# Attention heads with backward pass: the loads of K, V and wo on Activation's queue at written places, and half of the scale factors of Q made by VectorE

## The chip, the cores and the metric

The program runs on one core of a Trainium2 chip. It has a matrix engine (TensorE, PE in the rows of the profile), three engines for element-wise work (VectorE or DVE, Activation or ACT, GpSimd or POOL), and SyncE (SP), which issues transfers. DMAs are issued by SyncE, Activation or POOL; each has a queue of its own, and all run on the same sixteen DMA engines of the core. In the profile q1 is SyncE's queue, q0 POOL's and q10 Activation's. The metric is the device time of one execution in microseconds (us).

## The reference

One forward and backward pass of a block: layer norm of x (2048 rows of 576), attention of 32 heads over a cached K and V (2048 rows of 128 per head), a gated unit of width 4608, and their product added to x. All gradients are wanted.

```python
def _A_ref(x, k_cache, v_cache, wq, wo):
    q = (x @ wq).reshape(B, Sq, H, Dh).transpose(0, 2, 1, 3)
    scores = einsum("bhqd,bhkd->bhqk", q, k_cache) * (Dh ** -0.5)
    p = softmax(scores)
    o = einsum("bhqk,bhkd->bhqd", p, v_cache)
    return o.transpose(0, 2, 1, 3).reshape(B, Sq, H * Dh) @ wo
...
    xn = _layernorm(x)
    s = _A_ref(xn, k_cache, v_cache, wq, wo)
    g = silu(_B_ref(xn, w_gate, w_up, w_down))
    return x + s * g
```

The change lies in the attention heads. For each head the kernel computes the scores S = Q K^T, P = exp(S - max), the output O = P V divided by the sum of each row, dP = dO V^T, dS = P (dP - delta), and from them dQ = dS K, dK = dS^T Q and dV = P^T dO.

## The kernel before

The kernel first does the layer norm and the gated unit, then the 32 heads one after the other, then the products with wo, the gradients of the weights and dx. The heads are one long list of steps with positions, written by hand: `at(position, function, arguments)`. A head is 64 positions long, called halves (`HEAD`); head h starts at 64 h (`b`), and `back(x)` is position x of the head before. In halves 0 to 31 the score tiles are made, two halves for each of 16 blocks of 128 query rows (`s_half`, on VectorE line 523; `s_exp`, line 533); in halves 32 to 63 the tiles of dP and dS (`dp_half`, lines 554 to 560; `ds_mul`, line 564). These are the anchors; all else is put between them and overlaps with the next head.

The list is sorted and run through once. For TensorE, VectorE and Activation its order is the order in which they work (`MAN`). POOL and SyncE are not in `MAN`: a scheduler of the framework places their instructions, so the position of a step that POOL carries out says only where it stands in the list.

Within a head:

- `trans_P` and `trans_dS` turn pairs of finished blocks of P and dS by a DMA transpose that SyncE issues (line 568), 16 per head, into four buffers (`wpt`). The matmuls of `row_mm` (line 597) read them, in groups of four blocks: P with `Vn` from half 16.8 + 8 g on, dS with `Kn` from half 48.8 + 8 g on, so that the last two groups of dS run in the first halves of the next head.
- `kv_mm` (line 621) makes dV from P and the scaled dO (`dOn`), and dK from dS and the scaled Q (`Qn`). dV's two passes come first.
- `prep_kt` and `prep_vt` turn K and V on TensorE (line 485). K of the next head is turned at halves 37.2 and 40.0, V at halves 0.2 and 10.4 of its own head, eight of its sixteen blocks each time.
- `prep_wo` (lines 465 and 466) turns the head's part of wo at half 52.2 of the head before; `proj` makes Q and dO of the head from wq, wo and the inputs.
- `q_scale` multiplies Qn by 1/sum and the constant `SCALE`, eight blocks at a time, at halves 24.5 and 43.3: first the factors `rsc` (line 510, 128 x 8 numbers), then the product (line 511). Both run on POOL.
- `o_sink` finds delta: a product on POOL, its sum on VectorE, `negdelta` on POOL (line 657), which Activation uses in the first half of each block's dP (line 560).
- POOL also issues the stores of dV, dK, O and dQ (lines 634, 637, 659 and 669), 16 per head of 128 KB each.

The loads for the next head stand at `back(20.0)` (wq, line 449, and wo_h, line 454) and `back(35.1)` (K, line 425, and V, line 438), all issued by POOL. `Kn` has two buffers, used by even and odd heads; `Vn` and `wo_h` have one. So K waits for the last dQ matmul of the head before last, V for the last P V matmul of the head, wo_h for `prep_wo`. Head 0 has its K and V loaded in halves during the phase before (`LOADS`), line 419. In the last head Activation loads the rest of wo (`load_wo`, line 401), 15 DMAs.

Of the kernel before, what the change touches and what calls it, by code (L numbers as in the profile page):

```python
# [14 lines left out]
P = 128  # L15
# [81 lines left out]
def kernel(  # L97
# [6 lines left out]
    nc = tc.nc  # L104
# [6 lines left out]
    NT = S // P  # L111
# [8 lines left out]
    SCALE = float(Dh) ** -0.5  # L120
# [69 lines left out]
    wo_h = pk.tile([P, D], bf, name="wo_h")  # L190
# [186 lines left out]
    def bcast(v, n):  # L377
        return v.unsqueeze(2).to_broadcast([P, n, P])
# [4 lines left out]
    def at(pos, fn, *args):  # L383
        prog.append((pos, len(prog), fn, args))

    def anchor(pos, fn, *args):
        anchors.append((pos, len(anchors), fn, args))
# [25 lines left out]
            self.PT = [None] * NT  # L413
            self.dST = [None] * NT

    def load_part(dst, src, k):
        for k_ in range(2) if k is None else (k,):
            ts = slice(k_ * NT // 2, (k_ + 1) * NT // 2)
            nc.gpsimd.dma_start(dst[:, ts, :], src.rearrange("(p t) d -> p t d", t=NT)[:, ts, :])

    def load_k(hs, k=None):
        if not k:
            hs.Kn = (late["ldK2"] if hs.h % 2 else ldK).tile([P, NT, P], bf, name="Kn")
        if k is None:
            nc.gpsimd.dma_start(hs.Kn[:], A_k_cache[0, hs.h].rearrange("(p t) d -> p t d", t=NT))
        else:
            load_part(hs.Kn, A_k_cache[0, hs.h], k)

    def load_v(hs, k=None):
        if not k:  # L430
            hs.Vn = ld1.tile([P, NT, P], bf, name="Vn")
            hs.rs_all = hstat.tile([P, NT], f32, name="rs_all")
            hs.rinv_all = hstat.tile([P, NT], f32, name="rinv_all")
            hs.delta = hstat.tile([P, NT], f32, name="delta")
            hs.negdelta = hstat.tile([P, NT], f32, name="negdelta")
            hs.rsc = hstat.tile([P, NT], f32, name="rsc")
        if k is None:
            nc.gpsimd.dma_start(hs.Vn[:], A_v_cache[0, hs.h].rearrange("(p t) d -> p t d", t=NT))
        else:
            load_part(hs.Vn, A_v_cache[0, hs.h], k)  # L440

    def load_kv(hs):
        load_k(hs)
        load_v(hs)

    def load_wq(hs):
        hc = slice(hs.h * P, (hs.h + 1) * P)
        hs.wq = wh.tile([P, DT, P], bf, name="wq_h", bufs=1)
        nc.gpsimd.dma_start(hs.wq[:, :DL, :], A_wq[:DL * P, hc].rearrange("(t p) c -> p t c", p=P))
        nc.gpsimd.dma_start(hs.wq[:KL, DL, :], A_wq[DL * P:, hc])  # L450
        nc.gpsimd.memset(hs.wq[KL:, DL, :], 0.0)

    def load_wo_h(hs):
        nc.gpsimd.dma_start(wo_h[:], A_wo[hs.h * P:(hs.h + 1) * P, :])

    def load_w(hs):
        load_wq(hs)
        load_wo_h(hs)

    def prep_wo(hs, eng):  # L460
        hs.woT = wh.tile([P, DT, P], bf, name="woT_h", bufs=1)
# [45 lines left out]

    def q_scale(hs, g):
        gs = slice(g * 8, (g + 1) * 8)
        nc.gpsimd.tensor_scalar(hs.rsc[:, gs], hs.rinv_all[:, gs], SCALE, None, op0=ALU.mult)  # L510
        nc.gpsimd.tensor_tensor(hs.Qn[:, gs, :], hs.Qn[:, gs, :], bcast(hs.rsc[:, gs], 8), op=ALU.mult)

    def s_half(hs, qt, hf):
# [88 lines left out]
    def rows(pos, hs, T, rhs, g, sinks, w):  # L602
        bx = Box()
        sink, after = sinks
        for j in range(GQ):
            for kt in range(NT):
                at(pos + w * (j * NT + kt) / (GQ * NT - 1), row_mm, bx, hs, T, rhs, g * GQ + j, kt, sink)
        if after:
            at(pos + w + (DELTA1 if g == 1 else AFTER), after)
# [33 lines left out]
    def o_sink(hs, g):  # L643
        gs = slice(g * GQ, (g + 1) * GQ)
        bx = Box()

        def sink(acc):
            bx.ou = late["wt"].tile([P, GQ, P], bf, name="ou", bufs=1)
            alt.copy(bx.ou[:], acc[:], eng=OUE)
            bx.prod = late["wt"].tile([P, GQ, P], f32, name="prod", bufs=1)  # L650
            nc.gpsimd.tensor_tensor(bx.prod[:], bx.ou[:], hs.dOn[:, gs, :], op=ALU.mult)

        def after():
            prod, ou = bx.prod, bx.ou
            o_n = late["stg"].tile([P, GQ, P], bf, name="o_n", bufs=1)
            nc.vector.tensor_reduce(hs.delta[:, gs], prod[:], axis=AX.X, op=ALU.add)
            nc.gpsimd.tensor_scalar(hs.negdelta[:, gs], hs.delta[:, gs], -1.0, None, op0=ALU.mult)
            nc.gpsimd.tensor_tensor(o_n[:], ou[:], bcast(hs.rinv_all[:, gs], GQ), op=ALU.mult)
            nc.gpsimd.dma_start(on2_d[g * CH:(g + 1) * CH, hs.h * P:(hs.h + 1) * P].rearrange("(t p) d -> p t d", p=P), o_n[:])

        return sink, after
# [127 lines left out]
    HEAD = 2 * H1  # L789
    XR, ROW_W, ROW_W2, DELTA1 = 16.8, 6.7, 6.15, 5.7  # L790
    KVE, OUE = ("vs", "ss"), "s"
    WOT_AT = 52.2
    QT_AT, DOT_AT = ((32.6, 47.2, 55.2, 60.2), "s"), ((2.2, 6.2, 14.2, 18.2), "s")
    KT_AT, DON_AT, VT_AT, QN_AT = (37.2, 40.0, "s"), (8.9, 22.0, "v"), (0.2, 10.4, "s"), (24.2, 28.2, "s")
    PSTEP, QS_AT = 0.4, (24.5, 43.3)
# [7 lines left out]
    def adds(pos, w):  # L803
        load_[int(pos * FINE) % (HEAD * FINE)] += w
# [3 lines left out]
    for j in range(DT):  # L808
        adds(WOT_AT, 1)
    for p_ in KT_AT[:2] + DON_AT[:2] + VT_AT[:2] + QN_AT[:2]:  # L810
# [54 lines left out]
    for h in range(H):  # L865
        hs = Head(h) if h else first
        b = h * HEAD
        back = lambda x: b - HEAD + x
        if h:
            at(back(20.0), load_w, hs)  # L870
            at(back(35.1), load_kv, hs)
        for c in range(NCH):
            for i in range(DT):
                if h:
                    at(back(QT_AT[0][c] + PSTEP * i), proj, hs, "QT", c, i, QT_AT[1])
                at(b + (DOT_AT[0] if h else DOT_0)[c] + PSTEP * i, proj, hs, "dOT", c, i, DOT_AT[1])
        if h:
            at(back(WOT_AT), prep_wo, hs, "s")
        for g in range(2):
            if h:  # L880
                at(back(KT_AT[g]), prep_kt, hs, g, KT_AT[2])
            at(b + (DON_AT if h else DON_0)[g], prep_don, hs, g, DON_AT[2])
            at(b + (VT_AT if h else VT_0)[g], prep_vt, hs, g, VT_AT[2])
            at(b + QN_AT[g], prep_qn, hs, g, QN_AT[2])
            at(b + QS_AT[g], q_scale, hs, g)
        for p in range(NT // 2):
            at(b + 4 * p + 2 + RINV_AT, s_rinv, hs, p)
            at(b + max(4 * p + 2.1 + RINV_AT, DON_AT[p // 4] + 0.5), s_scale, hs, p)
        for qt in range(NT):
            p1, p2 = b + 2 * qt, b + H1 + 2 * qt  # L890
            for hf in range(NHF):
                anchor(p1 + hf, s_half, hs, qt, hf)
                anchor(p2 + hf, dp_half, hs, qt, hf)
            at(p1 + EXP_AT, s_exp, hs, qt)
            if qt % 2:
                if h == H - 1 and qt - 1 in P_PE:
                    for i, p_ in enumerate(P_PE[qt - 1]):
                        at(b + p_, pe_pair, hs.PT, hs.Pp, qt - 1, "PT", 8, ps_tr, "tr", i, "s")
                else:
                    at(p1 + PT_AT if h else max(p1 + PT_AT, LATE_AT + 0.1), trans_P, hs, qt - 1)  # L900
                if h == H - 1 and qt - 1 in DS_PE:
                    for i, p_ in enumerate(DS_PE[qt - 1]):
                        if len(DS_PE[qt - 1]) == 4:
                            at(b + p_, pe_pair, hs.dST, hs.dSp, qt - 1, "dST", 8, ps_tr, "tr", i, "s")
                        else:
                            at(b + p_, pe_pair, hs.dST, hs.dSp, qt - 1, "dST", NT, late["ps_big"], "big", i, "sv"[i])
                else:
                    at(p2 + DST_AT, trans_dS, hs, qt - 1)
            if qt not in STT2:
                at(p2 + DSM_AT, ds_mul, hs, qt)  # L910
        for g in range(NG):
            rows(b + 8 * g + XR + (0 if h or g else O0), hs, hs.PT, "Vn", g, o_sink(hs, g), ROW_W - (0 if h or g else O0))
            rows(b + H1 + 8 * g + XR, hs, hs.dST, "Kn", g, dq_sink(hs, g), ROW_W2 if g == 2 else ROW_W)
        for half, (pv, pk_) in enumerate(((VA, KA), (VB, KB))):
            kv(b, pv, hs, hs.P, "dOn", half, dvT_d, out_3)
            kv(b, pk_, hs, hs.dS, "Qn", half, dkT_d, out_2)
# [18 lines left out]
    if True:  # L935
# [84 lines left out]
        with tc.tile_pool(name="b1o", bufs=2, reuse_waits="tile") as outp, tc.tile_pool(name="b1t", bufs=3, reuse_waits="tile") as tmpp, \  # L1020
# [17 lines left out]
            class halves:  # L1038
                n, t = 0, None
# [298 lines left out]
```

## Time and profile before

| | us |
|---|---|
| three runs | 4982.95, 4999.9, 5007.65 |
| median | 4999.9 |
| the profiled execution | 4992.16 |
| its span, from the first to the last instruction | 4990.4 |

The granted clock of TensorE over the span is 0.997. Of the parts, the heads take the most: the first score tile of head 0 is worked on at 452.3 us, the last matmul of the last head's dQ starts at 3603.1 us.

How to read the rows: an engine's busy time is the sum of its instructions; a row of instructions has the line in the kernel, the engine, the operation, output and inputs by their names, the count, busy time and mean duration, and in a timeline the start and the duration in us, with the idle time before it and what ended it in brackets. A row of windows has for each engine the busy time and in brackets the number of instructions. A row of one line's instructions gives shortest, median and longest in ns and the first and last start in us.

### The profile page before, as it was taken

The page shows a single profiled execution, that of the slowest core. Times are in us where ns is not written, and L with a number is a line of the kernel's source. Part 1 is how long each engine was busy: PE and PEld are TensorE (multiplying, and loading weights), DVE is VectorE, ACT ScalarE, POOL GpSimd, SP SyncE. Part 2 cuts the span into 40 slices and gives each one's busy share as a digit, 9 for nine tenths or more (in the row PEclk, how much of TensorE's full clock was granted, in tenths as well). Part 3 has the DMA queues.
Part 4 walks back from the last instruction along what each step waited for, and adds up shares of the span by engine and source line. Part 5 has one row for each costly group of instructions (what it writes and reads, how often), then busy time and mean ns, then how long its engine had stood idle before and what let it go on. Part 6 is the DMA issues. An engine that isn't in the chain of part 4 may idle for free.

```text
span 4990.4 us, 103082 instructions
## 1 busy us (share of the span) xinstructions
PE 4886.3 (98%) x43022; PEld 3079.7 (62%) x43760; DVE 3072.9 (62%) x4844; ACT 2475.2 (50%) x3135; POOL 1543.3 (31%) x2206
## 2 busy tenths in 40 slices
PE   9999999999999999999999999999999999999999
PEld 3445776666666666666666666666657777655554
DVE  6545878888887888888787887887632222110111
ACT  5534666766666676676666666766502222100000
POOL 4323333333343333334333333333323332211000
PEclk9999999999999999999999999999999999999999
DMA  7887999999999999999999999999999989999898
GB/s 258 279 221 153 206 206 209 209 213 207 206 214 213 210 208 207 206 208 207 209 211 202 210 209 202 206 209 204 224 202 258 248 230 249 279 271 240 185 229 196
DMA packets 2879845, 1086.91 MB, mean 218 GB/s; under 512 B 2685360, under 2 KB 2808240, under 8 KB 2879376
## 3 DMA queue, kind: packets, MB, share of 16 engines
q1 hardware_dynamic: 2789728, 789.32, 87.9%
q0 software_dynamic: 85440, 286.38, 20.1%
q8 instruction: 342, 5.60, 0.5%
q10 hardware_dynamic: 4208, 4.57, 0.4%
q14 instruction: 127, 1.04, 0.1%
HBM read 172.54 MB, written 231.41 MB: 81 GB/s over the span
## 4 chain that ended last, share of the span: by engine, by line
PE 81%; DMA 8%; issue 1%; DVE 0%; ACT 0%; POOL 0%; DVEq 0%; ACTq 0%; POOLq 0%
PE acc L597 18%; PE acckv L621 14%; PE sp L521 8%; PE acc L1266 8%; PE dp L554 7%; DMA dST<-dSq 5%; PE accw L1119 5%; PE accp L478 5%; PE accd L1093 3%; PE dh L1065 2%; PE acc L1185 2%; PE acc L1001 2%; PE acct L485 2%; PE accq L1196 2%; PE acckv L618 2%
## 5 line engine op out<-in xcount | busy, mean ns | idle before, releaser
L533 ACT ACTIVATE Pq<-sneg,nm 128x2048 bf16<-128x2048 bf16 x512 | 1025.7, 2003 | 227.4 <-DVE sneg L523 190.1
L597 PE MATMUL acc<-Kn,dST 128*128 128x128 bf16 x8192 | 937.8, 220 | 39.0 <-DMA dST<-dSq 23.9
L557 DVE SCALAR_TENSOR_TENSOR dSq<-dp,delta,Pq 128x1024 bf16<-128x1024 f32 x544 | 694.7, 1282 | 374.8 <-PE dp L554 371.9
L597 PEld LDWEIGHTS <-dST 128*128 128x128 bf16 x8192 | 669.5, 98 | 397.0 <-DMA dST<-dSq 32.8
L597 PE MATMUL acc<-Vn,PT 128*128 128x128 bf16 x8192 | 899.1, 219 | 13.2 <-DMA PT<-Pq 2.7
L597 PEld LDWEIGHTS <-PT 128*128 128x128 bf16 x8192 | 652.0, 98 | 348.5 <-DMA PT<-Pq 5.1
L560 ACT ACTIVATE t<-dp,negdelta 128x1024 bf16<-128x1024 f32 x480 | 535.1, 1115 | 487.5 <-PE dp L554 477.6
L523 DVE TENSOR_SCALAR_CACHE_REDUCE sneg<-sp,nm 128x1024 bf16<-128x1024 f32 x512 | 656.5, 1282 | 114.8 <-PE sp L521 98.7
L523 DVE TENSOR_SCALAR_CACHE_REDUCE sneg<-sp 128x1024 bf16<-128x1024 f32 x512 | 625.2, 1221 | 98.6 <-PE sp L521 54.1
L554 PE MATMUL dp<-VT,dOT 128*128 128x512 bf16 x1988 | 597.9, 380 | 3.0 <-DVE dSq L557 0.3
L521 PE MATMUL sp<-KT,QT 128*128 128x512 bf16 x1960 | 590.7, 379 | 3.4 <-DVE sneg L523 2.8
L621 PE MATMUL acckv<-dSq,Qn 128*128 128x512 bf16 x1739 | 587.9, 380 | 0.4 <-ACT kv L41 0.3
L621 PE MATMUL acckv<-Pq,dOn 128*128 128x512 bf16 x1681 | 553.5, 379 | 1.7 <-POOL dOn L541 0.3
L564 DVE TENSOR_TENSOR dSq<-t,Pq 128x1024 bf16<-128x1024 bf16 x480 | 377.6, 787 | 0.0
L541 POOL TENSOR_TENSOR dOn<-dOn,rinv_all 128x256 bf16<-128x256 bf16 x256 | 157.1, 614 | 368.3 <-DVE rinv_all L537 317.2
L1119 PEld LDWEIGHTS <-xn_all 128*128 128x128 bf16 x2304 | 224.2, 98 | 28.1 <-DMA xn_all<-xn_d 0.4
L1282 DVE SCALAR_TENSOR_TENSOR junk<-dxn,xn_all 128x576 f32<-128x576 f32 x16 | 12.1, 758 | 362.5 <-ACT dxn L1277 362.5
L1266 PEld LDWEIGHTS <-cf 128*128 128x128 bf16 x2304 | 145.5, 98 | 136.8 <-DMA wqT<-in_A_wq_dram 0.2
L521 PEld LDWEIGHTS <-QT 128*128 128x128 bf16 x2048 | 169.7, 98 | 95.9 <-issue 6.1
L554 PEld LDWEIGHTS <-dOT 128*128 128x128 bf16 x2048 | 169.9, 98 | 95.2 <-issue 5.8
L478 PE MATMUL accp<-xnT,wq_h 128*128 128x512 bf16 x612 | 220.4, 381 | 0.1
L1277 ACT ACTIVATE dxn<-acc 128x512 f32<-128x512 f32 (+1 forms) x32 | 12.8, 406 | 394.9 <-issue 302.1
(217 smaller groups left out, 7272.4 us busy)
## 6 DMA issues: line engine op xcount, KB each, us to landing
h_d<-h_row POOLq DMA_DIRECT2D x48, 384.0 KB, 2.7
a_d<-a_row POOLq DMA_DIRECT2D x48, 384.0 KB, 3.5
b_d<-b_row POOLq DMA_DIRECT2D x48, 384.0 KB, 4.5
a_blk<-a_d SPq DMA_DIRECT2D x18, 1024.0 KB, 6.4
b_blk<-b_d SPq DMA_DIRECT2D x18, 1024.0 KB, 21.8
out_dram<-turn SPq DMA_DIRECT2D x35, 512.0 KB, 4.0
h_blk<-h_d POOLq DMA_DIRECT2D x17, 1024.0 KB, 15.9
on_d<-o_n POOLq DMA_DIRECT2D x128, 128.0 KB, 6.4
```

Source lines behind the costliest of these rows:

```text
L478: nc.tensor.matmul(acc[:], lhsT=w[:, i, :], rhs=(srcT if i < DL else xnT)[:, i, cs], start=(i == 0), stop=(i == DL))
L521: nc.tensor.matmul(sp[:, c * CH:(c + 1) * CH], lhsT=hs.QT[:, qs], rhs=hs.KT[:, hf * HW_ + c * CH: hf * HW_ + (c + 1) * CH], start=True, st ...
L523: nc.vector.tensor_scalar(sneg[:, hf * HW_:(hf + 1) * HW_], sp[:], -SCALE, None if hf == 0 else nm[:, hf - 1:hf], op0=ALU.mult, op1=ALU.mi ...
L533: nc.scalar.activation(Pq, sneg[:], AF.Exp, bias=nm[:, hf:hf + 1], scale=-1.0, accum_out=hs.rs_all[:, qt:qt + 1])
L554: nc.tensor.matmul(dp[:, c * CH:(c + 1) * CH], lhsT=hs.dOT[:, qs], rhs=hs.VT[:, hf * HW_ + c * CH: hf * HW_ + (c + 1) * CH], start=True, s ...
L557: nc.vector.scalar_tensor_tensor(dSq[:, hsl], dp[:], hs.delta[:, qt:qt + 1], Pq[:, hsl], op0=ALU.subtract, op1=ALU.mult)
L560: nc.scalar.activation(t[:], dp[:], AF.Identity, bias=hs.negdelta[:, qt:qt + 1], scale=1.0)
L564: nc.vector.tensor_tensor(hs.dS[qt][:, hsl], t[:], hs.P[qt][:, hsl], op=ALU.mult)
L597: nc.tensor.matmul(bx.acc[:, j, :], lhsT=T[qt][:, kt, :], rhs=getattr(hs, rhs)[:, kt, :], start=(kt == 0), stop=(kt == NT - 1))
L621: nc.tensor.matmul(bx.acc[i][:], lhsT=w, rhs=slabs[qt][:, k0:k0 + CH], start=(qt == 0), stop=(qt == NT - 1))
L1119: nc.tensor.matmul(acc[:kd, :FB], lhsT=xn_all[:, st, d0:d0 + kd], rhs=blk_[:, st, :], start=(st == 0), stop=(st == NT - 1))
L1266: nc.tensor.matmul(accs[sl][j][:, :nn], lhsT=ch[:, kk, sl * P:(sl + 1) * P], rhs=w_[:, n0:n0 + nn], start=(pi == 0 and kk == 0), stop=(las ...
```

## The change

K and V of heads 1 to 31 are loaded in two halves (blocks 0 to 7 and 8 to 15, 256 KB each). They and wo_h (144 KB) are issued by Activation, each at a position of its own, in the order of the list: wo_h at half 30.3 of the head before, K at 18.3 and 26.3, V at 50.3 and 60.3. wq stays on POOL at 20.0. Head 0's loads stay on POOL as they are. The factors `rsc` of blocks 8 to 15 are made by VectorE instead of POOL, in its written order at half 43.3; the product with Qn stays on POOL and needs them. Functions and branches that nothing calls any more are gone.

```diff
-    def load_part(dst, src, k):
-        for k_ in range(2) if k is None else (k,):
+    def load_part(dst, src, k, eng=nc.gpsimd):
+        for k_ in (k,):
             ts = slice(k_ * NT // 2, (k_ + 1) * NT // 2)
-            nc.gpsimd.dma_start(dst[:, ts, :], src.rearrange("(p t) d -> p t d", t=NT)[:, ts, :])
+            eng.dma_start(dst[:, ts, :], src.rearrange("(p t) d -> p t d", t=NT)[:, ts, :])
...
-    def load_k(hs, k=None):
+    def load_k(hs, k, eng=nc.gpsimd):
         if not k:
             hs.Kn = (late["ldK2"] if hs.h % 2 else ldK).tile([P, NT, P], bf, name="Kn")
-        if k is None:
-            nc.gpsimd.dma_start(hs.Kn[:], A_k_cache[0, hs.h].rearrange("(p t) d -> p t d", t=NT))
-        else:
-            load_part(hs.Kn, A_k_cache[0, hs.h], k)
+        load_part(hs.Kn, A_k_cache[0, hs.h], k, eng)
...
-    def load_v(hs, k=None):
+    def load_v(hs, k, eng=nc.gpsimd):
...
-        if k is None:
-            nc.gpsimd.dma_start(hs.Vn[:], A_v_cache[0, hs.h].rearrange("(p t) d -> p t d", t=NT))
-        else:
-            load_part(hs.Vn, A_v_cache[0, hs.h], k)
...
+        load_part(hs.Vn, A_v_cache[0, hs.h], k, eng)
...
-    def load_wo_h(hs):
-        nc.gpsimd.dma_start(wo_h[:], A_wo[hs.h * P:(hs.h + 1) * P, :])
...
+    def load_wo_h(hs, eng=nc.gpsimd):
+        eng.dma_start(wo_h[:], A_wo[hs.h * P:(hs.h + 1) * P, :])
...
-        nc.gpsimd.tensor_scalar(hs.rsc[:, gs], hs.rinv_all[:, gs], SCALE, None, op0=ALU.mult)
+        (nc.vector if g else nc.gpsimd).tensor_scalar(hs.rsc[:, gs], hs.rinv_all[:, gs], SCALE, None, op0=ALU.mult)
         nc.gpsimd.tensor_tensor(hs.Qn[:, gs, :], hs.Qn[:, gs, :], bcast(hs.rsc[:, gs], 8), op=ALU.mult)
...
-    WOT_AT = 52.2
+    WOT_AT, WOH_AT, KN_AT, VN_AT = 52.2, 30.3, (18.3, 26.3), (50.3, 60.3)
...
         if h:
-            at(back(20.0), load_w, hs)
-            at(back(35.1), load_kv, hs)
+            at(back(20.0), load_wq, hs)
+            at(back(WOH_AT), load_wo_h, hs, nc.scalar)
+            for k in range(2):
+                at(back(KN_AT[k]), load_k, hs, k, nc.scalar)
+                at(back(VN_AT[k]), load_v, hs, k, nc.scalar)
```

More of the change, by code (lines that the diff above doesn't have):

```diff
@@ L436, in load_v @@
             hs.rsc = hstat.tile([P, NT], f32, name="rsc")
-        if k is None:
-            nc.gpsimd.dma_start(hs.Vn[:], A_v_cache[0, hs.h].rearrange("(p t) d -> p t d", t=NT))
-        else:
-            load_part(hs.Vn, A_v_cache[0, hs.h], k)
-    def load_kv(hs):
-        load_k(hs)
-        load_v(hs)
+        load_part(hs.Vn, A_v_cache[0, hs.h], k, eng)
     def load_wq(hs):
@@ L451, in load_wq @@
         nc.gpsimd.memset(hs.wq[KL:, DL, :], 0.0)
-    def load_wo_h(hs):
[L454 to L458, printed above, removed]
+    def load_wo_h(hs, eng=nc.gpsimd):
+        eng.dma_start(wo_h[:], A_wo[hs.h * P:(hs.h + 1) * P, :])
     def prep_wo(hs, eng):
```

## The prediction

> **What bounds the kernel now.** First the page, for the engines and the queues.
>
> ```profile
> PE 4886.3 (98%) x43022; PEld 3079.7 (62%) x43760; DVE 3072.9 (62%) x4844; ACT 2475.2 (50%) x3135; POOL 1543.3 (31%) x2206
> ...
> q1 hardware_dynamic: 2789728, 789.32, 87.9%
> ```
>
> TensorE is busy 98% of the span; behind it stands the queue of SyncE (q1), which carries the transposes of P and dS. All that the change touches runs once per head, so next I cut the heads out of the trace: head 15, the three worst, heads 1 and 2, heads 3 to 30 together, and the last.
>
> ```profile
> core 0: us, PE busy (x) PEld busy (x) DVE busy (x) ACT busy (x) POOL busy (x), PEclk, DMA share, GB/s
> 1916.30:2013.00 96.70, 95.83 (x863) 61.50 (x878) 79.56 (x117) 65.45 (x74) 34.74 (x48) 1.00 1.17 211
> 2305.90:2406.60 100.70, 97.53 (x863) 62.18 (x878) 79.68 (x117) 65.56 (x74) 34.76 (x48) 0.98 1.16 209
> 2600.30:2701.70 101.40, 97.65 (x863) 62.19 (x878) 79.56 (x117) 65.55 (x74) 34.74 (x48) 0.98 1.19 200
> 3290.80:3393.90 103.10, 98.62 (x862) 62.67 (x877) 79.91 (x117) 65.47 (x74) 34.32 (x48) 0.97 1.20 201
> 550.70:749.60 198.90, 193.45 (x2484) 155.02 (x2524) 159.15 (x233) 130.91 (x147) 69.50 (x95) 1.00 1.19 206
> 749.60:3490.60 2741.00, 2693.73 (x24237) 1728.96 (x24685) 2226.45 (x3249) 1832.97 (x2045) 970.11 (x1313) 1.00 1.17 208
> 3490.60:3587.60 97.00, 93.39 (x872) 60.97 (x887) 79.50 (x116) 67.59 (x73) 30.85 (x40) 1.00 1.22 221
> ```
>
> A good head takes 96.70 us and TensorE never stops in it: that is its floor, and the change removes no matmul. One half is 96.70/64 = 1.511 us, and half x of head 15 is at 1916.30 + 1.511x. Heads 3 to 30 take 2741.0, which is 33.4 above 28 floors; heads 1 and 2 are 5.5 above two. So **38.9 us are all that can be won here**. The waits of TensorE in heads 3 to 30 say for what:
>
> ```profile
> PE acc L597 <- DMA dST<-dSq: 20.6, 17, 3.6
> PE acc L597 <- DMA PT<-Pq: 1.5, 3, 0.6
> ```
>
> Columns: total us, times, longest. Nearly all is a late transpose of dS. The lost 33.4 are more than the 22.1 waited, since the clock stands at 0.97 to 0.98 in the bad heads. Where the worst waits lie:
>
> ```profile
> 2392.56 0.23 PE L597 MATMUL acc<-Kn,dST 128*128 128x128 bf16 x1 [2.27 <-DMA dST<-dSq]
> 2686.81 0.29 PE L597 MATMUL acc<-Kn,dST 128*128 128x128 bf16 x1 [2.14 <-DMA dST<-dSq]
> 3384.33 0.61 PE L597 MATMUL acc<-Kn,dST 128*128 128x128 bf16 x4 [3.60 <-DMA dST<-dSq]
> ```
>
> Less their heads' starts these are halves 57.3, 57.2 and 61.9: the second group of dS rows. The three heads alone hold 4.0 + 4.7 + 6.4 = 15.1 of the 33.4. Now SyncE, in head 15 and over the run:
>
> ```profile
> 1927.13 46.12 SPq L568 DMA_TRANSPOSE PT<-Pq  x8
> 1973.35 50.50 SPq L568 DMA_TRANSPOSE dST<-dSq  x8
> ...
> L568 SPq DMA_TRANSPOSE PT<-Pq x255: 4478/5691/10785, 464.9 to 3541.2; - x128
> L568 SPq DMA_TRANSPOSE dST<-dSq x254: 4801/5890/12525, 513.8 to 3584.7; - x127
> ```
>
> Sixteen transposes stand end to end for 96.62 of the 96.70 us. This **queue is as full as TensorE**; what slows it anywhere makes a later pair late, until a calmer stretch lets the queue catch up. What else uses the DMA engines (columns: count, size, median us from issue to landing). Each head stores on four times, and by the source dq, dK and dV four times too in the same size; the last two rows are the first head's loads, which are in halves already:
>
> ```profile
> on_d<-o_n POOLq DMA_DIRECT2D x128, 128.0 KB, 6.4
> Kn<-in_A_k_cache_dram POOLq DMA_DIRECT2D x31, 512.0 KB, 6.3
> Vn<-in_A_v_cache_dram POOLq DMA_DIRECT2D x31, 512.0 KB, 6.4
> wo_h<-in_A_wo_dram POOLq DMA_DIRECT2D x32, 144.0 KB, 5.5
> Kn<-in_A_k_cache_dram POOLq DMA_DIRECT2D x2, 256.0 KB, 5.1
> Vn<-in_A_v_cache_dram POOLq DMA_DIRECT2D x2, 256.0 KB, 4.9
> ```
>
> **The change part by part.** When the moved steps run now, in head 15:
>
> ```profile
> 1939.82 0.59 POOL L425 DMA_DIRECT2D Kn<-in_A_k_cache_dram  x1 [2.13 <-PE accp L478]
> ...
> 1970.15 1.90 POOL L511 TENSOR_TENSOR Qn<-Qn,rsc 128x1024 bf16<-128x1024 bf16 x1
> ...
> 1983.05 0.58 POOL L657 TENSOR_SCALAR negdelta<-delta 128x4 f32<-128x4 f32 x1 [3.05 <-DVE delta L656]
> ...
> 1987.84 0.59 POOL L438 DMA_DIRECT2D Vn<-in_A_v_cache_dram  x1 [4.21 <-PE acc L597]
> ...
> 1995.36 0.59 POOL L454 DMA_DIRECT2D wo_h<-in_A_wo_dram  x1
> ```
>
> These are halves 15.6 (K), 47.3 (V) and 52.3 (wo_h), whatever the positions 20.0 and 35.1 in the source say.
>
> *Loads, placing.* Before the pairs that are late at halves 57 to 62, V and wo_h now put 512 + 144 = 656 KB on the DMA engines; after the change it is V's first 256 KB (half 50.3), so 400 KB less. Price: the second 256 KB of a load adds 6.3 - 5.1 = 1.2 (K) to 6.4 - 4.9 = 1.5 us (V). 400 KB are thus 1.9 to 2.3 us; against waits of 2.27, 2.14 and 3.60 that lifts about 6.3 of 8.0, some three quarters: 11 of the 15.1. Of the other 18.3 + 5.5 I cannot say how much lies there: between none and all; I take a third, 8, as V's second half comes back at 60.3 in front of the third group. Gain 19, bounds 0 and 38.9.
>
> *Loads, new collisions.* 256 KB of K at 26.3 and wo_h at 30.3 now meet transposes of P. Those waits were 1.5 us in 28 heads, so there is room; I take 2 us, bounds 0 and 8 (the 400 KB's 2.1 us once in every eighth head).
>
> *Loads, number.* Two more DMAs per head. Eight shortest transposes of each kind are 8 x 4.478 + 8 x 4.801 = 74.2; 96.7 less that leaves 22.5 for everything else. POOL's 21 transfers (16 stores, K, V, wo_h and the two parts of wq, together 576 x 128 numbers of 2 bytes) carry 16 x 128 + 2 x 512 + 144 + 144 = 3360 KB, at 1.35 us per 256 KB 17.7 us. The 4.8 left are at most 0.23 us per DMA: two of them 0.46 per head, 14 us in 31 heads. From below nothing; I take 8, a little over the middle because the queue is full.
>
> The Trainium skill (DMA: Bandwidth & Descriptors, "Anatomy of one DMA") gives a transfer about 2.0 us fixed plus bytes at 436 GB/s, an estimate of 5.2 us for two halves against 3.2 for one load. Were the fixed part occupancy, the change would cost about 31 x 4 = 124 us; but 21 x 2.0 = 42 us would not fit the 22.5 that the transposes leave, and the page itself puts the fixed part down to completion latency, so I give this no chance.
>
> *Loads, issue.* Activation issues five per head; its own queue does so in the last head only:
>
> ```profile
> L401 ACTq DMA_DIRECT2D xnT<-in_A_wo_dram x8: 374/374/422, 3490.0 to 3534.6; - x8
> L401 ACTq DMA_DIRECT2D dsT<-in_A_wo_dram x7: 374/374/415, 3540.3 to 3576.4; - x7
> ```
>
> 5 x 0.374 = 1.9 us in an engine busy 65.45 of 96.70: nothing. Fifteen such loads fit in the last head, which ran at 97.00. New waits: K's first half at 18.3 (1943.95) waits for matmuls that were done at 1939.82, V's at 50.3 (1992.30) for some done at 1987.84. Both are past by 4 us. If not, what queues behind on Activation are the exponentials, or the copies of dp and of QT, and TensorE waits for those; the price is the wait itself.
>
> *Needed by.* Landing takes 5 to 7 us; the readers stand here:
>
> ```profile
> 1972.20 0.61 PE L485 MATMUL acct<-ident,Kn 128*128 128x128 bf16 x8
> ...
> 1994.34 0.39 PE L465 MATMUL acct<-ident,wo_h 128*128 128x128 bf16 x4
> ...
> 1996.81 0.38 PE L621 MATMUL acckv<-dSq,Qn 128*128 128x512 bf16 x1
> ...
> 2011.76 0.61 PE L485 MATMUL acct<-ident,Vn 128*128 128x128 bf16 x8
> ```
>
> K's halves go at 1943.95 and 1956.0, wo_h at 1962.1, V's at 1992.3 and 2007.4 (its second half is read from half 74.4 by the source, 2028.7): 16 us or more to spare everywhere.
>
> *Scale factors.* The second half of Qn is scaled from 1970.15 now; bound to VectorE at 43.3 it starts at about 1982. Its first reader can't be before 1996.81, so 12 us remain. VectorE there:
>
> ```profile
> 1982.87 0.68 DVE L564 TENSOR_TENSOR dSq<-t,Pq 128x1024 bf16<-128x1024 bf16 x1
> 1984.08 1.28 DVE L557 SCALAR_TENSOR_TENSOR dSq<-dp,delta,Pq 128x1024 bf16<-128x1024 f32 x1 [0.53 <-PE dp L554]
> ```
>
> A 128x8 operation is not among VectorE's rows; it lies between nothing and the 0.68 of the 128x1024 above, and fits the 0.53 us gap or spills 0.15 into it: nothing on the path, 32 x 0.15 = 5 us if there were no gap later. On POOL the 1.90 us can hold up negdelta (1983.05) to about 1985; it is for the rows from half 48, 1988.8. Nothing, then, and nothing won either.
>
> **Sum.** -19 + 2 + 8 = -9 us. The profiled execution took 4992.16 (span 4990.4 and 1.76 around it), so 4983 by its own time; the median of the three runs is 7.7 higher, 4999.9, and the late transposes differ from run to run. I put the 9 on the median: **4991**.
>
> **Rivals.** *A full queue gives nothing back (no change).* If the transposes are the bound over many heads, moving loads only moves the lateness, and the bytes are the same. For it: end to end, 96.62 of 96.70. Against: head 15 keeps its floor with the loads where they are. Time 4999.9 with nothing lost, to 5014 with the two DMAs' upper price.
>
> *All stalls go, or nearly all.* For: head 15's queue keeps up, so 2 us earlier may do for the rest. Then 4999.9 - 38.9 = 4961. Against: only 8.0 of the 22.1 us waited are shown to lie in the second group.
>
> *The loads on a queue of their own slow the transposes.* Now loads and stores share q0, one behind the other; on Activation's queue a load runs beside a store and a transpose. It decides from the point where every load makes its pair later than the 1.9 to 2.3 us won. Price: two more DMAs at the upper 14, and, if all five loads of a head are slowed as the last bytes of a load are (1.35 us for 256 KB) while they stand beside a store for a fifth of their time, 1168 KB x 1.35/256 x 0.2 = 1.2 us per head, 38 in all: 4999.9 + 14 + 38 = 5052; without the first, 5038. The Trainium skill (DMA: Bandwidth & Descriptors, "Queues, rings and completion order") has each DMA engine take turns between queues, so a transpose would keep a third of it beside two others. In the last head, with its fifteen loads on Activation's queue, TensorE's waits for transposes were no more than
>
> ```profile
> PE acc L597 <- DMA PT<-Pq: 1.3, 2, 0.8
> ```
>
> and this speaks for a small price. Stalls on Activation would end on this side too.
>
> **Chances.** A measurement of this kernel tells about 0.5%, 25 us, from no change: below 4975 is faster, above 5025 slower. Forecast (up to 25 us faster) 0.33; no gain (up to 25 slower) 0.18; all or nearly all stalls gone (over 25 faster) 0.27; slower by its own queue (over 25 slower) 0.22. So faster 0.27, within 0.51, slower 0.22. The range goes from 4950 (38.9 off, and 11 more by which runs vary) to 5040, between the fourth case's two prices; the likeliest case alone has 4975 to 5000.
>
> **What would show it.** Right: Activation issues K, V and wo_h at halves 18.3, 26.3, 30.3, 50.3 and 60.3, 0.37 us each and without a wait; the floor stays 96.70; waits for dS transposes fall under 20.6, and those at halves 57 to 62 first; Qn's second scaling starts near half 44. Wrong: waits for dS or P grow; the longest transposes exceed 12.5 us; Activation waits for matmuls ahead of a load; a head's floor changes.

## The result, and the profile after

The changed kernel takes **4971.77 us** (median of 20 runs, 4949.31 to 4992.14), the kernel before 4988.94 us (20 runs, 4977.19 to 5011.44). The ratio over all runs of both is 0.9961, with an interval of 0.995 to 0.9972 (it is not the quotient of the two medians, which is 0.9966): faster by 17 to 20 us, surely so, but by hardly more than 0.5% at most. The profiled execution of the changed kernel took 4981.1 us, with a span of 4979.3; that is 11.1 less than the span of before, and slower than 17 of its 20 runs.

The page of the changed kernel, for the engines and the three queues:

```profile
PE 4921.4 (99%) x43760; PEld 3079.2 (62%) x43760; DVE 3035.0 (61%) x4876; ACT 2474.1 (50%) x3135; POOL 1494.4 (30%) x2081
...
q1 hardware_dynamic: 2789728, 789.32, 88.9%
q0 software_dynamic: 75024, 249.30, 17.5%
q10 hardware_dynamic: 26528, 41.66, 3.4%
```

TensorE and SyncE's queue are as full as before; 41.66 MB now go by Activation's queue (q10), 4.57 before. (Of before, 738 matmul records are missing in the trace, 43022 for 43760, so the two busy times of PE aren't compared.) Now the heads, cut at their starts as before: a good head (13), two bad ones (6 and 28), heads 1 and 2, heads 3 to 30, the last head, and the rest; then the rest of before:

```profile
core 0: us, PE busy (x) PEld busy (x) DVE busy (x) ACT busy (x) POOL busy (x), PEclk, DMA share, GB/s
1718.80:1815.30 96.50, 96.50 (x879) 61.46 (x878) 78.37 (x118) 65.44 (x74) 33.16 (x44) 1.00 1.17 212
1035.00:1138.00 103.00, 98.28 (x879) 62.21 (x878) 78.30 (x118) 65.38 (x74) 33.10 (x44) 0.98 1.20 204
...
3172.70:3275.30 102.60, 98.75 (x882) 62.49 (x883) 78.49 (x119) 65.48 (x74) 33.21 (x44) 0.98 1.18 209
550.30:745.20 194.90, 194.90 (x2527) 155.10 (x2525) 156.72 (x236) 130.96 (x147) 66.37 (x87) 1.00 1.20 209
745.20:3468.20 2723.00, 2707.59 (x24685) 1726.37 (x24683) 2193.68 (x3277) 1831.93 (x2045) 926.89 (x1202) 1.00 1.19 209
3468.20:3568.50 100.30, 94.45 (x871) 61.03 (x870) 75.94 (x114) 66.64 (x73) 30.64 (x39) 0.97 1.18 212
3568.50:4979.30 1410.80, 1389.65 (x11920) 871.18 (x11917) 282.91 (x681) 176.08 (x423) 278.50 (x453) 1.00 1.03 234
```

```profile
3587.60:4990.40 1402.80, 1376.10 (x11739) 869.88 (x11898) 280.71 (x678) 175.28 (x422) 278.60 (x453) 1.00 1.00 235
```

Three things are to be seen. The floor of a head is 96.50, not 96.70. Heads 3 to 30 take 2723.0 for 2741.0, heads 1 and 2 take 194.9 for 198.9: 22.0 us won. And 11.3 of it are given back behind them: the last head 100.3 for 97.0, the rest, which the change doesn't touch, 1410.8 for 1402.8. In the last head TensorE waits for a late transpose of dS:

```profile
3490.41 0.40 PE L583 MATMUL acc<-Kn,dST 128*128 128x128 bf16 x2 [4.63 <-DMA dST<-dSq]
```

From the start of the last head to the end the 14 profiled executions of this study take 1495.3 to 1518.6 us, in no order that an edit would explain. A few waits of 4 to 8 us make most of the difference; all of them are for DMAs, mostly for O that is read back from memory (`oT` and `onb` from `on_d`). Why those are late now and then was not looked into. With 0.4 us less ahead of head 1, 22.0 + 0.4 - 11.3 = 11.1.

TensorE's waits in heads 3 to 30 (us, times, longest), and the two longest of them in the timeline:

```profile
PE acc L583 <- DMA dST<-dSq: 12.8, 6, 4.7
PE acc L583 <- ACT Pq L519: 1.1, 1, 1.1
PE acc L583 <- DMA PT<-Pq: 1.1, 2, 0.7
```

```profile
1044.74 0.23 PE L583 MATMUL acc<-Kn,dST 128*128 128x128 bf16 x1 [4.72 <-DMA dST<-dSq]
...
3181.97 0.23 PE L583 MATMUL acc<-Kn,dST 128*128 128x128 bf16 x1 [3.27 <-DMA dST<-dSq]
```

Waits for dS are 12.8 us in 6 waits, for 20.6 in 17. They also lie elsewhere: the two longest are at halves (1044.74 - 1035.00)/1.508 = 6.5 and 6.1, where the last groups of dS rows run. Over heads 1 to 31 the waits for dS at halves 56 to 63 went from 16.7 us (14) to 2.0 (2), those at halves 0 to 15 from 7.1 (6) to 15.5 (5), the 4.63 of the last head among them. So this one execution waits less often for dS, but not much less in sum.

The loads of one head on Activation's queue:

```profile
1745.88 0.33 ACTq L419 DMA_DIRECT2D Kn<-in_A_k_cache_dram  x1
1758.77 0.34 ACTq L419 DMA_DIRECT2D Kn<-in_A_k_cache_dram  x1
1765.22 0.33 ACTq L444 DMA_DIRECT2D wo_h<-in_A_wo_dram  x1
1793.87 0.33 ACTq L419 DMA_DIRECT2D Vn<-in_A_v_cache_dram  x1
1808.34 0.33 ACTq L419 DMA_DIRECT2D Vn<-in_A_v_cache_dram  x1
```

From the head's start at 1718.80 these are halves 18.0, 26.5, 30.8, 49.8 and 59.4, each 0.33 us with no wait in brackets.

### The profile page after: what moved, and what is told of

It is laid out like the page before. It is cut to its first block, busy times and chain, and to the rows that moved or that the text cites. A ratio compares the mean times of both kernels' runs of the same rounds, so it can differ in the third digit from the quotient of the medians.

```text
span 4979.3 us, 103882 instructions
## 1 busy us (share of the span) xinstructions
PE 4921.4 (99%) x43760; PEld 3079.2 (62%) x43760; DVE 3035.0 (61%) x4876; ACT 2474.1 (50%) x3135; POOL 1494.4 (30%) x2081
## 3 DMA queue, kind: packets, MB, share of 16 engines
q10 hardware_dynamic: 26528, 41.66, 3.4%
## 4 chain that ended last, share of the span: by engine, by line
PE 85%; DMA 4%; issue 1%; DVE 0%; ACT 0%; POOL 0%; SPq 0%; DVEq 0%; POOLq 0%; ACTq 0%
PE acc L583 18%; PE acckv L607 16%; PE sp L507 9%; PE dp L540 8%; PE acc L1255 8%; PE accp L464 5%; PE accw L1108 4%; PE accd L1082 3%; PE acc L1174 2%; PE dh L1054 2%; PE acc L990 2%; PE acct L471 2%; PE accq L1185 2%; DMA dST<-dSq 2%; PE acckv L604 2%
## 5 line engine op out<-in xcount | busy, mean ns | idle before, releaser
L583 PE MATMUL acc<-Kn,dST 128*128 128x128 bf16 x8192 | 936.5, 219 | 18.9 <-DMA dST<-dSq 17.4
L607 PE MATMUL acckv<-dSq,Qn 128*128 128x512 bf16 x1856 | 631.6, 381 | 0.3 <-ACT kv L41 0.3
L507 PE MATMUL sp<-KT,QT 128*128 128x512 bf16 x2048 | 611.4, 380 | 3.3 <-DVE sneg L509 2.8
L607 PE MATMUL acckv<-Pq,dOn 128*128 128x512 bf16 x1856 | 614.0, 379 | 0.4
L540 PE MATMUL dp<-VT,dOT 128*128 128x512 bf16 x2048 | 609.1, 379 | 0.4 <-DVE dSq L543 0.3
L550 DVE TENSOR_TENSOR dSq<-t,Pq 128x1024 bf16<-128x1024 bf16 x480 | 332.8, 693 | 0.0
L637 POOL TENSOR_TENSOR prod<-ou,dOn 128x512 f32<-128x512 bf16 x128 | 180.2, 1408 | 198.4 <-ACT ou L41 198.4
L1271 DVE SCALAR_TENSOR_TENSOR junk<-dxn,xn_all 128x576 f32<-128x576 f32 x16 | 12.1, 758 | 364.0 <-ACT dxn L1266 364.0
## 6 DMA issues: line engine op xcount, KB each, us to landing
b_blk<-b_d SPq DMA_DIRECT2D x18, 1024.0 KB, 21.7
h_blk<-h_d POOLq DMA_DIRECT2D x17, 1024.0 KB, 15.6
```

The lines of the kernel that those rows point to most:

```text
L507: nc.tensor.matmul(sp[:, c * CH:(c + 1) * CH], lhsT=hs.QT[:, qs], rhs=hs.KT[:, hf * HW_ + c * CH: hf * HW_ + (c + 1) * CH], start=True, st ...
L540: nc.tensor.matmul(dp[:, c * CH:(c + 1) * CH], lhsT=hs.dOT[:, qs], rhs=hs.VT[:, hf * HW_ + c * CH: hf * HW_ + (c + 1) * CH], start=True, s ...
L550: nc.vector.tensor_tensor(hs.dS[qt][:, hsl], t[:], hs.P[qt][:, hsl], op=ALU.mult)
L583: nc.tensor.matmul(bx.acc[:, j, :], lhsT=T[qt][:, kt, :], rhs=getattr(hs, rhs)[:, kt, :], start=(kt == 0), stop=(kt == NT - 1))
L607: nc.tensor.matmul(bx.acc[i][:], lhsT=w, rhs=slabs[qt][:, k0:k0 + CH], start=(qt == 0), stop=(qt == NT - 1))
```

## The experiments

Twelve kernels ran (there is no number 7), in three groups, each timed against the kernel before on the same chip: 4992.21 us (32 runs), 4991.12 (31) and 4989.29 (35). Each kernel's median is over 8 to 12 runs. The ratio is over all runs; the quotient of the medians differs from it by up to 0.17% (kernel 5: 0.9965 for 0.9982), so kernels are compared by the ratio and its interval. The table has the ratio with its interval, and from the one profiled execution the time of heads 3 to 30 and TensorE's waits in them for dS and for P, in us and times (dashes: none in that view).

| kernel | ratio | interval | heads 3-30 | dS | P |
|---|---|---|---|---|---|
| before | 1 | | 2741.0 | 20.6 (17) | 1.5 (3) |
| changed | 0.9961 | 0.995-0.9972 | 2723.0 | 12.8 (6) | 1.1 (2) |
| 1 no scale | 0.9967 | 0.9949-0.9985 | 2708.9 | 0.5 (1) | - |
| 2 scale only | 0.9993 | 0.9977-1.0008 | 2731.2 | 21.7 (21) | 0.9 (2) |
| 3 whole loads | 1.0016 | 0.9995-1.0036 | 2746.3 | 23.2 (15) | 11.7 (6) |
| 4 old places | 0.997 | 0.9953-0.9988 | 2724.9 | 16.8 (17) | - |
| 5 wo_h at old place | 0.9982 | 0.9957-1.0007 | 2721.9 | 5.7 (8) | 8.3 (5) |
| 6 halves on POOL | 1.006 | 1.0033-1.0087 | 2751.6 | 26.5 (27) | 7.1 (9) |
| 8 K whole | 1.0007 | 0.9983-1.003 | 2736.2 | 5.1 (8) | 18.2 (15) |
| 9 V whole | 0.9954 | 0.9936-0.9972 | 2703.2 | - | - |
| 10 queue only | 0.9973 | 0.9956-0.9989 | 2732.9 | 13.7 (12) | 3.3 (2) |
| 11 K whole, early | 0.9977 | 0.9958-0.9995 | 2712.3 | 5.0 (5) | 1.3 (1) |
| 12 wq on Activation | 0.9964 | 0.9944-0.9984 | 2702.2 | - | - |
| 13 K's halves together | 1.003 | 1.0009-1.0052 | 2743.3 | 18.9 (16) | 8.2 (8) |

**1. The changed kernel without the scale factors on VectorE.**

```diff
-        (nc.vector if g else nc.gpsimd).tensor_scalar(hs.rsc[:, gs], hs.rinv_all[:, gs], SCALE, None, op0=ALU.mult)
+        nc.gpsimd.tensor_scalar(hs.rsc[:, gs], hs.rinv_all[:, gs], SCALE, None, op0=ALU.mult)
```

> The changed kernel with one part undone: the factors of blocks 8 to 15 are made by POOL again, so that Qn's second half may be scaled from about half 35 on. Placing theory (the gain comes from the 400 KB that no longer stand before the second group of dS rows): the gain of 17 us stays nearly whole, 13 to 19 us under the kernel before; TensorE's waits at halves 57 to 62 stay near the 2 us of the changed kernel. Scale theory (POOL's product slows VectorE's products beside it, mean 787 ns before and 693 after, so dS is late): at most 6 us under the kernel before, and the 693 ns go back to about 787.

4979.16 us, ratio 0.9967: nearly all of the gain is there without that part. The floor of its heads is back at 96.70. In all four kernels in which POOL makes these factors (before, 1, 6 and 10) the shortest and commonest length of a head is 96.7 us, in the ten others 96.5.

**2. The kernel before with that line alone changed.**

> The kernel before with the factors of blocks 8 to 15 made by VectorE at half 43.3 and nothing else. Placing theory: 0 to 4 us under the kernel before, with the waits for dS at halves 57 to 62 about as before (some 17 us in all). Scale theory: 11 us or more under it, VectorE's product of dS near 693 ns, dS ready about 1 us earlier.

4984.95 us, 0.9993: about a fifth of the gain by the ratio, and by itself not told from nothing. Its good heads take 96.50. The timelines show how. In head 15 of before POOL's product of Qn runs from 1970.15 to 1972.05 (its row stands in the prediction). VectorE beside it:

```profile
1970.92 1.68 DVE L564 TENSOR_TENSOR dSq<-t,Pq 128x1024 bf16<-128x1024 bf16 x1
```

Head 13 of the changed kernel, at the same place and at the product's new place:

```profile
1773.43 0.68 DVE L550 TENSOR_TENSOR dSq<-t,Pq 128x1024 bf16<-128x1024 bf16 x1
...
1785.99 1.89 POOL L497 TENSOR_TENSOR Qn<-Qn,rsc 128x1024 bf16<-128x1024 bf16 x1
...
1787.59 0.84 DVE L550 TENSOR_TENSOR dSq<-t,Pq 128x1024 bf16<-128x1024 bf16 x1
```

VectorE's product of 0.68 us takes 1.68 when POOL's product runs beside it. Where POOL's product stands now, VectorE's meets only its end (0.84). Over all 480 of this form the page of before and that of the changed kernel have (busy us, mean ns):

```profile
L564 DVE TENSOR_TENSOR dSq<-t,Pq 128x1024 bf16<-128x1024 bf16 x480 | 377.6, 787 | 0.0
```

```profile
L550 DVE TENSOR_TENSOR dSq<-t,Pq 128x1024 bf16<-128x1024 bf16 x480 | 332.8, 693 | 0.0
```

The Trainium skill (GPSIMD Engine Reference, "1. Specifications") says that POOL shares its interfaces to the on-chip memory with VectorE, with contention where VectorE's instruction has two inputs from there; the row of 1.68 agrees. How this reaches TensorE: VectorE's next instruction on dp (line 543), and two neighbouring pairs of matmuls that make dp, in head 13 of kernel 1, which has POOL's factors (start 1716.0), and of the changed kernel (start 1718.8):

```profile
1772.82 1.27 DVE L543 SCALAR_TENSOR_TENSOR dSq<-dp,delta,Pq 128x1024 bf16<-128x1024 f32 x1
...
1772.95 0.59 PE L540 MATMUL dp<-VT,dOT 128*128 128x512 bf16 x2
...
1774.14 0.59 PE L540 MATMUL dp<-VT,dOT 128*128 128x512 bf16 x2
```

```profile
1774.86 1.28 DVE L543 SCALAR_TENSOR_TENSOR dSq<-dp,delta,Pq 128x1024 bf16<-128x1024 f32 x1
...
1775.76 0.59 PE L540 MATMUL dp<-VT,dOT 128*128 128x512 bf16 x2
...
1776.75 0.59 PE L540 MATMUL dp<-VT,dOT 128*128 128x512 bf16 x2
```

VectorE comes 56.82 and 56.06 us after the head's start, 0.76 earlier. The pairs stand 1.19 us apart in the one and 0.99 in the other; up to the first of them the heads run alike to 0.02 us, and behind it all is 0.2 us earlier. (The profile marks no wait at these matmuls; the chain is read from the starts.) By the floor the part is worth 31 x 0.2 = 6.2 us; the timed runs have about 3 (0.9961 against 0.9967, 0.9993 against 1), with intervals that hold both nothing and 6.2.

**3. The changed kernel with K and V whole, at 18.3 and 50.3.**

```diff
-            ts = slice(k_ * NT // 2, (k_ + 1) * NT // 2)
+            ts = slice(k_ * NT // 2, (k_ + 1) * NT // 2) if eng is nc.gpsimd else slice(0, NT)
...
-            for k in range(2):
-                at(back(KN_AT[k]), load_k, hs, k, nc.scalar)
-                at(back(VN_AT[k]), load_v, hs, k, nc.scalar)
+            at(back(KN_AT[0]), load_k, hs, 0, nc.scalar)
+            at(back(VN_AT[0]), load_v, hs, 0, nc.scalar)
```

> The changed kernel with K and V loaded whole by Activation at 18.3 and 50.3 (wo_h at 30.3): two DMAs fewer per head. If each DMA has a price of up to 0.23 us in the full queue: 7 to 14 us less from that; if the place of bytes decides: V's 512 KB at 50.3 put 256 KB back before the second group, 1.2 to 1.5 us later there and as much earlier in the third, so within 6 us of the changed kernel either way, with waits moving from halves 0 to 8 to halves 57 to 62.

5004.62 us, 1.0016: the whole gain is gone, though two DMAs fewer are issued per head. Neither of its two forecasts came: number doesn't set the price here, and the place of the bytes costs more than 6 us.

**4. Whole loads by Activation, at the places where POOL issued them.** Beside the edit of kernel 3 only the positions differ. wo_h comes one head late, so that this kernel makes dO from the wo of the head before.

```diff
-    WOT_AT, WOH_AT, KN_AT, VN_AT = 52.2, 30.3, (18.3, 26.3), (50.3, 60.3)
+    WOT_AT, WOH_AT, KN_AT, VN_AT = 52.2, 52.5, (15.9, 26.3), (47.8, 60.3)
```

> The changed kernel with K, V and wo_h whole, issued by Activation where POOL issued them before: halves 15.9, 47.8 and 52.5. Only the queue and the scale factors differ from the kernel before. Placing theory: no more than 5 us under the kernel before, waits for dS at halves 57 to 62 near 17 us again. Queue theory (loads off POOL's queue cost the transposes less): 13 us or more under it.

4979.14 us, 0.997: without halves and without the new places most of the gain is there. What is left of the change in this kernel is the queue and the scale factors.

**5. wo_h at its old place, two heads ahead.**

```diff
-    WOT_AT, WOH_AT, KN_AT, VN_AT = 52.2, 30.3, (18.3, 26.3), (50.3, 60.3)
+    WOT_AT, WOH_AT, KN_AT, VN_AT = 52.2, 52.5 - 64, (18.3, 26.3), (50.3, 60.3)
```

> The changed kernel with wo_h back at its old place, half 52.5 of the head before last, still issued by Activation; K and V stay in halves at their new places. Placing theory (every byte ahead of the second group of dS counts, 144 KB are 0.7 us there): 4 to 10 us slower than the changed kernel, TensorE's waits at halves 57 to 62 up from 2 to some 6 us. Piece theory (only a load of 512 KB in one go makes a pair later than its slack, smaller ones are absorbed): within 4 us of the changed kernel.

4973.47 us, 0.9982, an interval that holds both the changed kernel and no change. Its waits at halves 56 to 63 are 2.0 us: wo_h is not what made those pairs late in this profile; in time the two theories of the forecast can't be told apart.

**6. The kernel before with K and V in halves, back to back on POOL.**

```diff
     def load_kv(hs):
-        load_k(hs)
-        load_v(hs)
+        for k in range(2):
+            load_k(hs, k)
+        for k in range(2):
+            load_v(hs, k)
```

> The kernel before with K and V each in two DMAs of 256 KB, still issued by POOL, one right after the other where POOL issued them before (halves 15.6 and 47.3); the factors stay on POOL. Piece theory with the space between the halves as what matters: within 5 us of the kernel before. If the size of a DMA matters by itself: 12 us or more under it. If two more DMAs per head have the price of the prediction (up to 0.23 us each): 5 to 14 us over it.

5017.83 us, 1.006: 26.7 us slower by the medians (16 to 43 by the interval) with not a byte more, for 62 DMAs, 0.43 us each. None of the three forecasts went that high.

**8 and 9. The changed kernel with K whole at 18.3; with V whole at 50.3.** The edit of kernel 8 (that of 9 is the same for V), where k = 2 loads all blocks:

```diff
-                at(back(KN_AT[k]), load_k, hs, k, nc.scalar)
...
+            at(back(KN_AT[0]), load_k, hs, 2, nc.scalar)
```

> The changed kernel with K loaded whole at half 18.3, V in halves, wo_h at 30.3. Piece theory: TensorE's waits for transposes of P at halves 24 to 47 return (12 us in the run with both loads whole), those for dS at 57 to 62 stay near 2; 8 to 18 us slower than the changed kernel. If K's place and size are indifferent: within 4 us of it.

> The changed kernel with V loaded whole at half 50.3, K in halves, wo_h at 30.3. Piece theory: waits for dS at halves 56 to 63 return (23 us in the run with both loads whole), none for P; 15 to 25 us slower than the changed kernel. If only K's whole load was at fault there: within 5 us of the changed kernel.

K whole: 4989.08 us, 1.0007, the gain gone. V whole: 4966.32 us, 0.9954, nothing lost. So with the other load in halves, halving matters for K alone. What K whole costs is seen in TensorE's waits of heads 3 to 30, which turn from dS to P:

```profile
PE acc L583 <- DMA PT<-Pq: 18.2, 15, 2.5
PE acc L583 <- DMA dST<-dSq: 5.1, 8, 1.4
```

**10. The queue alone.** The kernel before with Activation in POOL's place, loads whole (k = 2), POOL making all factors.

```diff
-    WOT_AT = 52.2
+    WOT_AT, WOH_AT, KN_AT, VN_AT = 52.2, 52.5 - 64, (15.9,), (47.8,)
...
-            at(back(20.0), load_w, hs)
-            at(back(35.1), load_kv, hs)
+            at(back(20.0), load_wq, hs)
+            at(back(WOH_AT), load_wo_h, hs, nc.scalar)
+            at(back(KN_AT[0]), load_k, hs, 2, nc.scalar)
+            at(back(VN_AT[0]), load_v, hs, 2, nc.scalar)
```

> The kernel before with one thing changed: K, V and wo_h are issued by Activation, whole, at the places where POOL issued them (halves 15.9, 47.8, 52.5; wo_h two heads ahead). POOL makes all scale factors. If the queue alone is worth something (a load no longer stands in the same ring as the stores, ahead of or behind them): 8 to 15 us under the kernel before, ratio 0.997 to 0.9985, waits for dS at halves 56 to 63 still 10 us or more. If only places and halves count: ratio 0.9995 to 1.001. If a queue of its own slows the transposes: above 1.002.

4975.32 us, 0.9973: 14 us (5 to 22 by the interval), with the same loads of the same size at the same halves (15.5, 47.3 and 52.0 in its trace; 15.6, 47.3 and 52.3 before). POOL's stores stay where they were as well: in heads 3 to 29 each is issued at the same half to 0.1 (median), but for the last one of dQ, 0.4 earlier; so it isn't their places that changed. The loads land sooner, K in 5.5 us for 6.3 and V in 5.5 for 6.5 (medians over heads 3 to 30). By the medians this is the largest single part of the change. The waits in heads 3 to 30 are fewer, and in the same places as before (12.1 us of them at halves 56 to 63):

```profile
PE acc L583 <- DMA dST<-dSq: 13.7, 12, 2.3
PE acc L583 <- DMA PT<-Pq: 3.3, 2, 2.8
```

**11 and 13. K's place, and K's halves together.** The changed kernel with K whole (k = 2) at 15.9; with K's halves at 18.3 and 18.4. The positions of the one and the other:

```diff
-    WOT_AT, WOH_AT, KN_AT, VN_AT = 52.2, 30.3, (18.3, 26.3), (50.3, 60.3)
+    WOT_AT, WOH_AT, KN_AT, VN_AT = 52.2, 30.3, (15.9,), (50.3, 60.3)
...
+    WOT_AT, WOH_AT, KN_AT, VN_AT = 52.2, 30.3, (18.3, 18.4), (50.3, 60.3)
```

> The changed kernel with K loaded whole at half 15.9 in place of whole at 18.3 (which gave 1.0007) or in halves at 18.3 and 26.3 (0.996). If the place makes the load of K dear (at 18.3 it lands beside the same pair of transposes of P for which TensorE then waits): ratio 0.995 to 0.997, waits for P under 4 us. If 512 KB in one piece are dear at any place: 0.999 to 1.002, waits for P 10 us or more at halves 24 to 47.

> The changed kernel with K's two halves issued one right behind the other at half 18.3. If it is the eight halves between the two that make the halved load cheap (256 KB per pair of transposes): like K whole at 18.3, ratio 1.0 to 1.002, waits for P 10 us or more. If it is the size of one transfer (the ring takes turns between shorter ones): ratio 0.995 to 0.997, waits for P under 4 us.

K whole at 15.9: 4974.19 us, 0.9977, between its two forecasts, with waits for P of 1.3 us as the first had it. Halves together at 18.3: 5001.14 us, 1.003. So neither the size of a transfer nor the number decides, but where K's 512 KB land: from 18.3 in one go they cost 0.46% whole and 0.7% in halves (kernels 8 and 13 against the changed one, 23 and 34 us, the intervals lie apart); from 15.9, or with the second half eight halves later, they don't (the intervals of 8 and 11 overlap, but those of kernels 3 and 4, with all loads whole at the later and at the earlier places, lie apart). In the trace of 13 waits of both kinds come back:

```profile
PE acc L583 <- DMA dST<-dSq: 18.9, 16, 3.6
PE acc L583 <- DMA PT<-Pq: 8.2, 8, 2.9
```

Two stores of dK are issued at half 22.4 to 22.8 and one of O at 25.9, just behind a load from 18.3; that this is the collision was not tried.

**12. V whole, and wq by Activation at 22.3.**

```diff
-            at(back(20.0), load_wq, hs)
+            at(back(22.3), load_wq, hs, nc.scalar)
```

> The changed kernel with V whole at 50.3, and wq too issued by Activation, at half 22.3 in place of POOL's 61.2. wq's 144 KB then no longer stand ahead of the third group of dS rows. If bytes ahead of dS pairs are what makes them late, the median slack of pair 5 of dS grows by 1 us or more and the time stays or falls by up to 5 us: ratio 0.9935 to 0.9955. If P's pairs pay for it: waits for P 5 us or more and a ratio above 0.997.

4969.98 us, 0.9964, between its two forecasts. The foreseen slack is there: pair 5 of dS, counted from 0, lands at half 64.4 for 65.4 in kernel 9 (medians of heads 3 to 29), 1.5 us sooner. In its profile heads 3 to 30 wait for no transpose and take 2702.2, the floor of 28 x 96.5 = 2702.0; the timed runs don't tell it from the changed kernel or from kernel 9. With 4966.32 kernel 9 has the lowest median of all, also within what can be told of the changed one.

## Why the prediction came out as it did

Faster by 17 us where 9 were forecast, inside the range, and with 4971.77 just under the 4975 to 5000 of the likeliest case. (The 4991 started from a median of three runs, 4999.9, where twenty have 4988.94.) So direction and size came out about right, but in part by luck: the largest part of the gain, the queue, was put at nothing, and the terms that were to bring it, placing against number, come to about nothing in time.

- **The floor (96.70, unchanged): wrong.** It is 96.50. This is the step "Nothing, then, and nothing won either" of the scale factors, and the prediction itself has "a head's floor changes" among the signs of being wrong. It looked at whether the moved operation finds room, and not at what ran beside the old one: POOL's product at 1970.15 stands in the prediction, VectorE's 1.68 us beside it does not; the 0.68 was taken from another place of the head, although the mean of that form was 0.787. Worth 3 us (timed) to 6 (floor).
- **What would show it: all but the floor held.** Activation issues within a half of the places named (the last one, at 59.4, 0.9 ahead), without a wait; Qn's second product starts at 1785.99, half 44.6; waits for dS fell, those at halves 57 to 62 first.
- **Issue (nothing): wrong in what it left out.** The issue itself did cost nothing. But the step priced only Activation's 0.37 us per DMA and held the two queues to be alike; the queue alone (kernel 10) is worth 14 us. Activation's queue was a rival only as a loss (38 us). That rival has fallen: with the same loads beside stores and transposes TensorE waited 17.0 us for transposes in heads 3 to 30 (kernel 10), not 22.1.
- **Number (+8, bounds 0 to 14): wrong as one price.** On POOL's queue two more DMAs per head cost 27 us (kernel 6), above the upper bound; on Activation's, V's second DMA cost nothing that can be told (0.9961 and 0.9954).
- **Placing (-19) and new collisions (+2): the mechanism is there in the traces, its worth in time isn't shown.** Pair 3 of dS, the last that the second group needs, lands at half 59.7 in before, 58.7 in kernel 10 and 56.9 in kernel 1 (medians of heads 3 to 29): the new places and halves bring it 1.8 halves forward, 2.7 us, where 1.9 to 2.3 were estimated. Waits at halves 56 to 63 fell from 16.7 to 2.0 us, as foreseen, and only in kernels with the new places (5.1 us or less there in kernels 1, 5, 8, 9, 11, 12 and 13; 12.1 or more in 2, 4, 6, 10, and in 3, which has the new places with K and V both whole). But kernels 10 and 1, which differ by places and halves alone, have 0.9973 and 0.9967: in time 3 us, which can't be told from nothing. In the profiled executions it can: 2732.9 and 2708.9 for heads 3 to 30. Over the 14 kernels the timed medians mostly rise with that column of the table (4966 and 4970 us at 2703, 5001 to 5018 at 2743 to 2752), and kernels 10 and 1 are the pair that doesn't follow. One execution each is too little to settle which of the two is nearer.
- **The reason given for placing was half of it.** The 400 KB of V and wo_h were held to be what counts. V whole at 50.3 does as well (kernel 9), and so, as far as can be told, does wo_h at its old place (kernel 5); it is K that needs its halves, at the place that it was moved to.
- **A full queue gives nothing back: fallen,** as it does give back; **all stalls go (4961): not reached** (heads 1 to 30 still take 194.9 + 2723.0 = 2917.9, 22.9 over 30 floors of 96.50), though the heads of kernels 9 and 12 come near it.
- **Needed by (16 us or more to spare): miscounted, without effect.** V's first half goes at 1992.3 and is read from 2011.76; less the 5 to 7 us of landing that is 12 to 14 us. No load came late.

Step by step, from before by kernel 10 and kernel 1 to the changed kernel, the ratio goes 1, 0.9973, 0.9967, 0.9961: about 14 us for the queue, 3 for places and halves, 3 for the scale factors (6 by the floor). Only the first is more than the runs' noise. That places and halves come to so little fits with the halves paying for the new place of K.

Why POOL's queue is the dearer one is open. The Trainium skill (DMA: Bandwidth & Descriptors, "Issuing engines are not separate DMA queues") says that transfers of all issuers interleave on the same engines, and that several issuers save only the time of issuing. By that kernel 10 would have gained no more than POOL's time to issue, 0.59 us a load in an engine that is busy for 31% of the span; it measured 0.9973. The Trainium skill (DMA: Bandwidth & Descriptors, "SWDGE vs HWDGE vs iDMA") also says that for POOL's transfers software writes the descriptors into rings in SBUF, and that those of Activation and SyncE don't pass there. That fits the sign of kernels 6 and 10; no run here separates it from other causes.

## What to carry to other kernels

Before a load is halved or moved, try it at the same size and place on a hardware queue: here that was the larger part of the gain, and splitting on POOL's queue the largest loss. When a small operation is moved between engines, look at what its neighbour, released by it, runs beside: POOL's product next to VectorE's cost 1 us per head in a row that looked like a fixed duration. A place in a nearly full schedule is good or bad as a whole: K at 18.3 needed its halves, at 15.9 not.

## What the runs showed of the hardware

A long wait halves TensorE's clock for 3.4 or 6.8 us, so that a late transpose can cost more than the wait. Two waits in before, 3.60 us (to 3384.33) and 2.27 us (to 2392.56), and the stretches around them:

```profile
3376.20:3383.00 6.80, 4.47 (x40) 2.65 (x38) 3.63 (x4) 2.23 (x2) 0.00 (x0) 1.00 1.19 117
3383.00:3389.80 6.80, 5.47 (x26) 3.15 (x27) 1.88 (x2) 0.56 (x1) 0.30 (x1) 0.50 1.29 225
3389.80:3396.60 6.80, 6.75 (x62) 4.32 (x63) 4.93 (x8) 2.15 (x3) 1.98 (x4) 0.99 1.17 222
...
2393.20:2396.60 3.40, 3.40 (x17) 1.84 (x16) 1.88 (x2) 0.43 (x1) 0.00 (x0) 0.50 1.24 276
2396.60:2400.00 3.40, 3.35 (x34) 2.30 (x34) 1.79 (x2) 1.49 (x2) 0.00 (x0) 1.00 1.21 239
```

The column behind POOL's is the granted clock: 0.50 for 6.8 us, from 1.3 us ahead of the first wait's end, and for 3.4 us behind the second, then about 1.00; 17 matmuls in 3.4 us, then 34. In the 14 traces, from head 1 to 4900 us, none of about 180 waits of 0.6 to 2.07 us brought it, and 47 of the 62 from 2.10 to 7.86 us did, 32 times for 3.4 and 15 times for 6.8 us. The Trainium skill (TensorE: Matmul & The Clock Gate, "Part 1: The HAM clock gate") has the half clock come after an idle window of about 3.4 us and windows of 3413 ns that run free: the lengths agree, but here waits from 2.1 us on could be enough.
